# One addition per step moved from VectorE to an accumulating transfer, and the last whole-float32 products with w_out split in two

## The chip, the cores and the metric

The kernel runs on one core of a Trainium2 chip. The metric is the device time of one execution in microseconds (us); lower is better. Five engines matter here: TensorE (PE in the profile, its weight loads PEld), VectorE (DVE), ScalarE (ACT), GpSimd (POOL) and SyncE (SP). Each takes its instructions strictly in the order of the program and waits on semaphores for the others. SyncE and GpSimd here mostly issue transfers. Only GpSimd issues the transfers that add to their destination.

## The reference, cut to what matters

Attention over 8 batches and 8 heads gives `x` with 4608 rows and 512 columns. Behind it comes a feed-forward layer whose activation is a ratio of two polynomials:

```
h = x @ w_in                               # 4608x512 @ 512x2048
P = a[0] + a[1]*h + a[2]*h*h + a[3]*h*h*h  # the numerator
Q = 1 + |b[0]|*|h| + |b[1]|*h*h            # the denominator
g = P / (Q + 1e-6)
out = g @ w_out                            # 4608x2048 @ 2048x512
```

All inputs and outputs are float32.

## The kernel before, in words

The 4608 rows of `x` are cut into nine blocks of 512: eight hold the first 512 rows of a batch, the ninth the last 64 rows of all batches. A block takes 16 steps, one for each 128 columns of `h`, so there are 144 steps in all. Step n has three parts.

- H(n): TensorE makes 128 columns of `h` for the block's 512 rows, in one PSUM bank. In the first `NAT = 16` steps, which are block 0, it does so with whole float32 operands (L897): 4 instructions of the program, 8 records in the profile. From step 16 on both factors are split into a high and a low part, and three of the four products of the parts are summed (L909): 12 instructions.
- middle(n): four passes of ScalarE over the bank give `tb` = |b0 h|, `tq` = h², `ta` = a3 h + a2 and `u` = a1 h + a0. VectorE makes `tb` = b1 h² + |b0 h| (L937), `ta` = `ta` times `tq` (L942) and `ta` = `ta` + `u` (L943), which is P. ScalarE takes a logarithm and an exponential, `tq` = 1/Q. Then VectorE makes `gh` = `ta` times `tq` in the rounded format that TensorE takes at its faster rate (L949) and, in three more instructions (L952, L957, L958), the correction `gl`.
- O(n): TensorE multiplies `gh` and `gl` with the two parts of the matching 128 rows of w_out, 12 instructions (L989), and adds them to four PSUM banks that hold the block's output. In the first `WO = 4` steps it multiplies the whole float32 quotient with whole w_out instead: one VectorE instruction (L947) writes the quotient over `u`, and O(n) is 4 instructions (L970), 8 records.

The tiles are few and shared. Step n uses the set of its parity: `m0`, `m2`, `m4` are `ta`, `tb`, `tq` of even steps, `m1`, `m3`, `m5` of odd ones. `gb0` and `gb1` are `u`, and they are the same memory as `g0` and `g1`, which are `gh`; likewise `gb2`, `gb3` (the logarithm) and `g2`, `g3` (`gl`). So ScalarE can write `u` of step n only after O(n-2) has read `gh` of step n-2, and `ta` only after L957 of step n-2. H(n) alternates between two banks from step 2 on and needs its bank read out by all four passes of step n-2.

Around the steps runs the rest: attention for the coming block (its scores are L692, the pooled ones L467), the weights, which come as eight megabyte-sized loads for each of w_in and w_out (SP L344), each unpacked by one ScalarE and two VectorE instructions (L351, L354, L357) and split by one of each (L371, L374), and the pooled inputs of attention, which GpSimd sums by accumulating transfers (L419).

Every piece of work is entered in a list with its engine, an assumed duration, what it reads and writes, a due time and a lag until its readers can go on. A planner (`Plan.run`) plays this list through and takes the open task with the earliest latest start on each engine; its order is the order of the program. `H_FIRST` is the spacing of due times for the steps of block 0, `H_STEP` that of the others. In the lists below a name such as `g0_122` is tile `g0` with a number of the allocator; `wh1`, `wl1` and `wb1` are the high part, the low part and the whole of w_out, `wb0` the whole of w_in, `xf0_1` is `x` of block 0, `sx` and `sl` are places where loads land.

Of the kernel before, what the change touches and what calls it, by code (L numbers as in the profile page):

```python
# [14 lines left out]
ALU = mybir.AluOpType  # L15
# [9 lines left out]
POOL = 4  # L25
# [48 lines left out]
class Plan:  # L74
# [11 lines left out]
    def add(self, engine, dur, fn, reads=(), writes=(), due=None, lag=None):  # L86
        t = Task()
        t.engine, t.dur, t.fn, t.due, t.n = engine, dur, fn, due, len(self.tasks)
        t.lag, t.preds, t.succs, t.late, t.start = lag, {}, [], 1e9, None
        rk = set().union(*(r.keys for r in reads)) if reads else set()  # L90
        wk = set().union(*(w.keys for w in writes)) if writes else set()
        for k in rk | wk:
            w = self.writer.get(k)
            if w is not None:
                t.preds[w] = True
        for k in wk:
            for r in self.readers.get(k, ()):
                t.preds.setdefault(r, False)
            self.writer[k] = t
            self.readers[k] = []  # L100
        for k in rk - wk:
            self.readers[k].append(t) if k in self.readers else self.readers.__setitem__(k, [t])
        t.preds.pop(t, None)
        for p in t.preds:
            p.succs.append(t)
        self.tasks.append(t)
        return t
# [75 lines left out]
def attention_moe(  # L183
# [13 lines left out]
    nc = tc.nc  # L197
# [3 lines left out]
    add = plan.add  # L201
# [136 lines left out]
    def weights(w, f, spot, due=None):  # L338
# [26 lines left out]
        add("DVE", 1.13, lower, (spot, lo), (lo,))  # L365
        if f >= (WO if w else NAT):
            parts(w, f)

    def parts(w, f, due=None):
        hi, lo, word = high2[w][f // 2], low2[w][f // 2], bits2[w][f // 2]  # L370
        add("ACT", 0.88, lambda: nc.scalar.copy(out=hi.ap, in_=word.ap.bitcast(F32)), (lo,), (hi,), due=due)  # L371
        add(
            "DVE", 1.13,
            lambda: nc.vector.tensor_tensor(  # L374
                out=lo.ap, in0=word.ap.bitcast(F32), in1=hi.ap.bitcast(F32), op=ALU.subtract
            ),
            (lo, hi), (lo,), due=due,
        )
# [152 lines left out]
    def normalize(c):  # L531
# [22 lines left out]
        else:  # L554
            add("ACT", 0.92, pooled, (*c.eproom, s.sm), c.eproom, lag=LATE)
        add(
# [3 lines left out]
            ),  # L560
            (s.el, s.sm), (s.el,), lag=None if c.b == 0 else LATE,
        )
# [289 lines left out]
    def due_h(n):  # L852
        m = blocks[0].nstep
        return H0 + H_FIRST * min(n, m) + H_STEP * max(0, n - m)

# [26 lines left out]
    def bank_h(n):  # L882
        return banks[HFIRST[n]] if n < len(HFIRST) else hb[n % 2]
# [37 lines left out]
    def act(cost, out_, room_in, in_, func, *more, **kw):  # L921
        add("ACT", cost, lambda: nc.scalar.activation(out=out_.ap, in_=in_, func=func, **kw), (room_in, cf, *more), (out_,))  # L922

    def middle(n):

        ta, tb, tq = (mt[2 * i + n % 2] for i in range(3))
        gh, gl = gt[n % 2], gt[2 + n % 2]
        u, log = gb[n % 2], gb[2 + n % 2]
        h = bank_h(n)
        act(0.58, tb, h, h.ap, AF.Abs, scale=b0)  # L930
        act(0.48, tq, h, h.ap, AF.Square)
        act(0.66, ta, h, h.ap, AF.Identity, scale=a3, bias=a2)
        act(0.66, u, h, h.ap, AF.Identity, scale=a1, bias=a0)
        v = nc.vector
        add(
            "DVE", 0.66,
            lambda: v.scalar_tensor_tensor(  # L937
                out=tb.ap, in0=tq.ap, scalar=b1, in1=tb.ap, op0=ALU.mult, op1=ALU.add
            ),
            (tq, tb, cf), (tb,),  # L940
        )
        add("DVE", 0.61, lambda: v.tensor_tensor(out=ta.ap, in0=ta.ap, in1=tq.ap, op=ALU.mult), (ta, tq), (ta,))  # L942
        add("DVE", 0.61, lambda: v.tensor_tensor(out=ta.ap, in0=ta.ap, in1=u.ap, op=ALU.add), (ta, u), (ta,))  # L943
        act(0.63, log, tb, tb.ap, AF.Ln, bias=cone)
        act(0.54, tq, log, log.ap, AF.Exp, scale=-1.0)
        if n < WO:
            add("DVE", 0.61, lambda: v.tensor_tensor(out=u.ap, in0=ta.ap, in1=tq.ap, op=ALU.mult), (ta, tq), (u,))  # L947
            return
        add("DVE", 0.61, lambda: v.tensor_tensor(out=gh.ap, in0=ta.ap, in1=tq.ap, op=ALU.mult), (ta, tq), (gh,))  # L949
        add(  # L950
            "DVE", 0.61,
            lambda: v.scalar_tensor_tensor(  # L952
                out=tb.ap, in0=tb.ap, scalar=CONE, in1=gh.ap.bitcast(F32), op0=ALU.add, op1=ALU.mult
            ),
            (tb, gh), (tb,),
        )
        add("DVE", 0.61, lambda: v.tensor_tensor(out=tb.ap, in0=ta.ap, in1=tb.ap, op=ALU.subtract), (ta, tb), (tb,))  # L957
        add("DVE", 0.61, lambda: v.tensor_tensor(out=gl.ap, in0=tb.ap, in1=tq.ap, op=ALU.mult), (tb, tq), (gl,))  # L958

    def o_part(n, f):  # L960
# [4 lines left out]
        due = due_h(n) + O_LAG * H_STEP + 0.25 * f  # L965
        if n < WO:
            for sub in range(blk.nsub):
# [120 lines left out]
    for n in range(NS + LAG):  # L1088
        if n < NS:
            k, s = steps[n]  # L1090
            for f in range(blocks[k].fg):
                h_part(n, f)
                if n < NAT:
                    if n % 2:
                        parts(0, n - 1, due_h(n - 1 + blocks[0].nstep) - 2.0)
                    if n == NAT - 1 and NAT < blocks[0].nstep:
                        split_x(0, due_h(NAT) - 3.0)
            if s == blocks[k].nstep - 1:

                if k + 1 < len(blocks):  # L1100
                    split_x(k + 1)
        o = n - LAG
        if o >= 0:
            k, s = steps[o]
            for f in range(blocks[k].fg):
                o_part(o, f)
            if s == blocks[k].nstep - 1:
                store(k)
                if blocks[k].b is not None and blocks[k].b + 2 < B:
                    attend(blocks[k].b + 2)  # L1110

        if n < NS:
            middle(n)
# [10 lines left out]
    for t in pe:  # L1124
        n = int(WARM * (t.start - end) / 0.107)
# [18 lines left out]
LAG = 2  # L1144
O_LAG = 2.11
H0 = 7.65
H_FIRST = 7.02
H_STEP = 6.3
SPLIT_EARLY = 9.51
QUAD_GAP = 37.85  # L1150
WARM = 0.6
EP_DVE = (0,)
WO = 4
SPOTS = (0, 1, 2, 3, 4, 5)
LATE = 1.2


_OUTS = [((NT, DM), "float32")]
# [65 lines left out]
```

## Time and profile before

| what | us |
|---|---|
| median of 3 runs | 971.54 (971.37 to 972.34) |
| time of the profiled execution | 972.59 |
| its span, first to last instruction | 970.70 |
| PE busy | 945.7 (97%) |
| DVE busy | 847.4 (87%) |
| ACT busy | 817.8 (84%) |
| POOL busy | 112.2 (12%) |

The span is the time that the profile covers; 1.89 us of the profiled execution lie around it. A timeline row gives start, busy time, engine, source line, operation, tiles and shape, and how many instructions were merged; a bracket tells how long the engine was idle before it and what ended that. Successive records of one engine overlap in these rows, so the price of an instruction is the distance between starts, not the busy time.

### The profile page before, as it was taken

The numbers are of one execution on the slowest core, as the hardware profiler recorded it, in microseconds if no ns is written. First come the engines' busy times: TensorE is split into PE (matmuls) and PEld (weight loads), VectorE is DVE, ScalarE is ACT, GpSimd is POOL, SyncE is SP. The second block draws the span as 40 slices with busy tenths as digits, with TensorE's granted clock in tenths as the row PEclk, the third lists the DMA queues.
The fourth block names the chain that finished last, engine by engine and source line by source line (L and its number), as shares of the span: only waits on it lengthen the run. The fifth ranks groups of instructions, "written<-read, shape, count | busy, mean of one in ns | idle before, by whom it ended". The sixth has DMA issues, their size and how long they took to land.

```text
span 970.7 us, 19136 instructions
## 1 busy us (share of the span) xinstructions
PE 945.7 (97%) x7077; PEld 738.4 (76%) x7077; DVE 847.4 (87%) x1438; ACT 817.8 (84%) x2054; POOL 112.2 (12%) x135
## 2 busy tenths in 40 slices
PE   4999999999999999999999999999999999999996
PEld 3745656887887788778877888778877888888885
DVE  5789999999897989898988889798989899988885
ACT  5799998998879897889788988988798977778774
POOL 1210121021202120112102210212021000000000
PEclk7799999999999999999999999999999999999998
DMA  9994463235424433344223532344242010001001
GB/s 311 273 330 136 110 152 62 94 57 120 78 77 75 107 57 93 81 98 78 68 96 55 122 72 83 60 119 66 71 94 63 1 44 1 1 1 44 1 1 44
DMA packets 43013, 84.85 MB, mean 87 GB/s; under 512 B 4872, under 2 KB 25736, under 8 KB 42920
## 3 DMA queue, kind: packets, MB, share of 16 engines
q1 hardware_dynamic: 25256, 63.42, 19.7%
q0 software_dynamic: 17664, 20.21, 15.2%
q8 instruction: 56, 0.92, 0.4%
q14 instruction: 37, 0.30, 0.1%
HBM read 74.17 MB, written 9.44 MB: 86 GB/s over the span
## 4 chain that ended last, share of the span: by engine, by line
PE 53%; DVE 22%; ACT 17%; issue 5%; DMA 2%; DVEq 0%; ACTq 0%
PE psum L989 23%; PE psum L909 21%; ACT el L727 5%; ACT m L922 5%; DVE g L949 3%; DVE m L952 3%; DVE m L957 3%; PE psum L605 2%; ACT gb L922 2%; DVE g L958 2%; DVE m L942 2%; DMA qk<-in_qk_dram 2%; DVE m L937 2%; DVE m L943 2%; ACT epc L523 2%
## 5 line engine op out<-in xcount | busy, mean ns | idle before, releaser
L989 PE MATMUL psum<-wh,g 128*128 128x512 f32 x1120 | 379.4, 401 | 1.8 <-DVE g L958 1.7
L909 PE MATMUL psum<-xs,wh 128*128 128x512 f32 x1024 | 261.6, 395 | 0.1
L922 ACT ACTIVATE m<-psum,cf 128x512 f32<-128x512 f32 x288 | 211.9, 741 | 58.5 <-PE psum L909 54.9
L989 PEld LDWEIGHTS psum<-wh,g 128*128 128x128 f32 x1120 | 208.0, 188 | 53.8 <-DVE g L958 4.7
L909 PEld LDWEIGHTS psum<-xs,wh 128*128 128x128 f32 x1024 | 189.3, 188 | 43.6 <-issue 2.9
L989 PE MATMUL psum<-wl,g 128*128 128x512 f32 x560 | 218.0, 390 | 0.0
L949 DVE TENSOR_TENSOR g<-m,m 128x512 fp32r<-128x512 f32 x140 | 96.6, 690 | 72.5 <-ACT m L922 66.7
L909 PE MATMUL psum<-xs,wl 128*128 128x512 f32 x512 | 137.0, 389 | 0.0
L922 ACT ACTIVATE gb<-psum,cf 128x512 f32<-128x512 f32 x144 | 114.9, 798 | 15.4 <-PE psum L989 15.4
L922 ACT ACTIVATE gb<-m,cf 128x512 f32<-128x512 f32 x144 | 106.4, 739 | 22.0 <-DVE m L937 19.7
L989 PEld LDWEIGHTS psum<-wl,g 128*128 128x128 f32 x560 | 105.2, 188 | 21.8 <-issue 1.4
L419 POOL DMA_DIRECT2D pq<-in_qkp_dram x84 | 73.7, 922 | 398.7 <-DMA pq<-in_qkp_dram 385.5
L922 ACT ACTIVATE m<-gb 128x512 f32<-128x512 f32 x144 | 92.6, 643 | 24.7 <-DVE m L942 22.5
L909 PEld LDWEIGHTS psum<-xs,wl 128*128 128x128 f32 x512 | 96.1, 188 | 20.3
L937 DVE SCALAR_TENSOR_TENSOR m<-m,cf,m 128x512 f32<-128x512 f32 x144 | 107.3, 745 | 1.6 <-ACT m L922 1.6
L943 DVE TENSOR_TENSOR m<-m,gb 128x512 f32<-128x512 f32 x144 | 98.9, 687 | 7.0 <-DVE m L942 0.5
L952 DVE SCALAR_TENSOR_TENSOR m<-m,g 128x512 f32<-128x512 f32 x140 | 96.5, 690 | 3.7
L942 DVE TENSOR_TENSOR m<-m,m 128x512 f32<-128x512 f32 x144 | 98.4, 683 | 0.0
L958 DVE TENSOR_TENSOR g<-m,m 128x512 fp32r<-128x512 f32 x140 | 95.8, 685 | 2.8
L957 DVE TENSOR_TENSOR m<-m,m 128x512 f32<-128x512 f32 x140 | 96.2, 687 | 2.1
L727 ACT ACTIVATE el<-el,nm 128x64 f32<-128x64 f32 x280 | 93.4, 340 | 2.8 <-DVE nm L721 2.8
L922 ACT ACTIVATE m<-psum 128x512 f32<-128x512 f32 x144 | 87.0, 604 | 0.0
(84 smaller groups left out, 924.9 us busy)
## 6 DMA issues: line engine op xcount, KB each, us to landing
qk<-in_qk_dram SPq DMA_DIRECT2D x32, 590.0 KB, 3.9
pq<-in_qkp_dram POOLq DMA_DIRECT2D x84, 144.0 KB, 3.3
vw<-in_vw_dram SPq DMA_DIRECT2D x32, 320.0 KB, 3.8
out_dram<-xf SPq DMA_DIRECT2D x32, 256.0 KB, 2.6
vpc<-in_vp_dram POOLq DMA_DIRECT2D x42, 168.0 KB, 3.8
sx<-in_w_in_dram SPq DMA_DIRECT2D x5, 1024.0 KB, 13.4
sl<-in_w_out_dram SPq DMA_DIRECT2D x4, 1024.0 KB, 7.0
sx<-in_w_out_dram SPq DMA_DIRECT2D x4, 1024.0 KB, 4.9
```

The lines of the kernel that those rows point to most:

```text
L419: lambda d=dst, x=x: nc.gpsimd.dma_start(out=d.ap, in_=x, accum_op=ALU.add),
L727: nc.scalar.activation(out=e[:, n], in_=e[:, n], func=AF.Exp, bias=nm[:, n : n + 1], scale=scale, accum_out=sm[:, n : n + 1],)
L909: nc.tensor.matmul(ph.ap[:, f * t : (f + 1) * t], lhsT=(high, low)[j][0][fc].ap[:, c, :], rhs=blk.x[i].ap[:, c, :] if blk.b is not None el ...
L922: add("ACT", cost, lambda: nc.scalar.activation(out=out_.ap, in_=in_, func=func, **kw), (room_in, cf, *more), (out_,))
L937: lambda: v.scalar_tensor_tensor(out=tb.ap, in0=tq.ap, scalar=b1, in1=tb.ap, op0=ALU.mult, op1=ALU.add),
L942: add("DVE", 0.61, lambda: v.tensor_tensor(out=ta.ap, in0=ta.ap, in1=tq.ap, op=ALU.mult), (ta, tq), (ta,))
L943: add("DVE", 0.61, lambda: v.tensor_tensor(out=ta.ap, in0=ta.ap, in1=u.ap, op=ALU.add), (ta, u), (ta,))
L949: add("DVE", 0.61, lambda: v.tensor_tensor(out=gh.ap, in0=ta.ap, in1=tq.ap, op=ALU.mult), (ta, tq), (gh,))
L952: lambda: v.scalar_tensor_tensor(out=tb.ap, in0=tb.ap, scalar=CONE, in1=gh.ap.bitcast(F32), op0=ALU.add, op1=ALU.mult),
L957: add("DVE", 0.61, lambda: v.tensor_tensor(out=tb.ap, in0=ta.ap, in1=tb.ap, op=ALU.subtract), (ta, tb), (tb,))
L958: add("DVE", 0.61, lambda: v.tensor_tensor(out=gl.ap, in0=tb.ap, in1=tq.ap, op=ALU.mult), (tb, tq), (gl,))
L989: nc.tensor.matmul(ob[sub].ap, lhsT=g[i].ap[:, f0 : f0 + P], rhs=flat((high, low)[j][1][fc].ap), start=(fc == 0 and m == 0), stop=(fc == N ...
```

## The change

In steps 0 to 15 the VectorE addition `ta` + `u` becomes a transfer, issued by GpSimd, that adds `u` to `ta`; the planner is told 0.95 us on GpSimd and a lag of 4.0 us. `WO = 0` makes O(0) to O(3) split products, with the four VectorE instructions for `gh` and `gl`, and has the parts of their w_out rows made when the weights are unpacked. `H_FIRST` becomes 6.39. The source lines behind the change move by 3.

```
-        add("DVE", 0.61, lambda: v.tensor_tensor(out=ta.ap, in0=ta.ap, in1=u.ap, op=ALU.add), (ta, u), (ta,))
+        if n < UN:
+            add("POOL", 0.95, lambda: nc.gpsimd.dma_start(out=ta.ap, in_=u.ap, accum_op=ALU.add), (ta, u), (ta,), lag=ULAG)
+        else:
+            add("DVE", 0.61, lambda: v.tensor_tensor(out=ta.ap, in0=ta.ap, in1=u.ap, op=ALU.add), (ta, u), (ta,))
...
-H_FIRST = 7.02
+H_FIRST = 6.39
...
-WO = 4
+WO = 0
...
+ULAG = 4.0
+UN = 16
```

On TensorE, before, the end of H(0) to H(3) is followed by O(0) and O(1) in whole float32, with the scores of attention between them, and then by the first half of H(4):

```order
L897 MATMUL psum<-xf0_1_107,wb0_2_75 128x512 x6
L970 MATMUL psum<-wb1_0_89,gb0_126 128x512 x4
L692 MATMUL psum<-qk0_148 64x64 x20
L970 MATMUL psum<-wb1_0_89,gb1_127 128x512 x4
L897 MATMUL psum<-xf0_1_107,wb0_4_77 128x512 x2
```

The same place on TensorE now (three equal pairs on `g0_122` and three on `g1_123` follow those shown, and are left out):

```order
L897 MATMUL psum<-xf0_1_107,wb0_2_75 128x512 x6
L692 MATMUL psum<-qk0_148 64x64 x20
L992 MATMUL psum<-wh1_0_64,g0_122 128x512
L992 MATMUL psum<-wl1_0_88,g0_122 128x512
L992 MATMUL psum<-wh1_0_64,g2_124 128x512 x4
L992 MATMUL psum<-wh1_0_64,g1_123 128x512
L992 MATMUL psum<-wl1_0_88,g1_123 128x512
L897 MATMUL psum<-xf0_1_107,wb0_4_77 128x512 x2
L992 MATMUL psum<-wh1_0_64,g3_125 128x512 x4
```

The scores moved ahead of O(0), and O(0) now needs `gh` first and `gl` (`g2_124`) before O(1) and H(4) can come.

On VectorE, before, the middle of steps 0 and 1, from the first addition to the second quotient:

```order
L943 TENSOR_TENSOR m0_116<-m0_116,gb0_126 128x512
L374 TENSOR_TENSOR wl0_0_72<-wb0_0_73,wh0_0_56 128x1024
L947 TENSOR_TENSOR gb0_126<-m0_116,m4_120 128x512
L937 SCALAR_TENSOR_TENSOR m3_119<-m5_121,cf_134,m3_119 128x512
L942 TENSOR_TENSOR m1_117<-m1_117,m5_121 128x512
L937 SCALAR_TENSOR_TENSOR m2_118<-m4_120,cf_134,m2_118 128x512
L943 TENSOR_TENSOR m1_117<-m1_117,gb1_127 128x512
L354 TENSOR_SCALAR wb1_2_91<-sl2_183 128x1024
L947 TENSOR_TENSOR gb1_127<-m1_117,m5_121 128x512
```

The same stretch on VectorE now, from the two products to `gl` of step 0:

```order
L942 TENSOR_TENSOR m0_116<-m0_116,m4_120 128x512
L937 SCALAR_TENSOR_TENSOR m2_118<-m4_120,cf_134,m2_118 128x512
L942 TENSOR_TENSOR m1_117<-m1_117,m5_121 128x512
L374 TENSOR_TENSOR wl0_0_72<-wb0_0_73,wh0_0_56 128x1024
L937 SCALAR_TENSOR_TENSOR m3_119<-m5_121,cf_134,m3_119 128x512
L952 TENSOR_TENSOR g0_122<-m0_116,m4_120 128x512
L354 TENSOR_SCALAR wb1_2_91<-sl2_183 128x1024
L955 SCALAR_TENSOR_TENSOR m2_118<-m2_118,g0_122 128x512
L357 SCALAR_TENSOR_TENSOR wb1_2_91<-sl2_183,wb1_2_91 128x1024
L960 TENSOR_TENSOR m2_118<-m0_116,m2_118 128x512
L952 TENSOR_TENSOR g1_123<-m1_117,m5_121 128x512
L961 TENSOR_TENSOR g2_124<-m2_118,m4_120 128x512
```

Both L943 are gone, four instructions for `gh` and `gl` stand in place of one L947, and two instructions of the weights as well as `gh` of step 1 stand between `gh` and `gl` of step 0.

On GpSimd the transfers of steps 0 to 5 now stand among those of attention:

```order
L419 DMA vpc_162<-in_vp_dram 112x384
L944 DMA m0_116<-gb0_126 128x512
L944 DMA m1_117<-gb1_127 128x512
L419 DMA vpc_162<-in_vp_dram 112x384
L944 DMA m0_116<-gb0_126 128x512
L944 DMA m1_117<-gb1_127 128x512
L944 DMA m0_116<-gb0_126 128x512
L419 DMA pq0_149<-in_qkp_dram 128x288
L419 DMA pq1_156<-in_qkp_dram 128x288
L944 DMA m1_117<-gb1_127 128x512
```

The row ahead of the first L944 is the second accumulation of `vpc`; that of step 5 stands behind the first ones of `pq0` and `pq1`, the second half of attention.

## The prediction, made before the changed kernel ran

> **What bounds the kernel now.** I read the page first, then the table by stage, then TensorE's timeline through block 0, then the engines that feed it.
>
> ```profile
> PE 945.7 (97%) x7077; PEld 738.4 (76%) x7077; DVE 847.4 (87%) x1438; ACT 817.8 (84%) x2054; POOL 112.2 (12%) x135
> 41.00:65.00 24.00, 23.98 (x222) 13.18 (x217) 17.63 (x29) 19.46 (x32) 5.16 (x6) 1.00 1.02 328
> 65.00:83.00 18.00, 18.00 (x81) 8.17 (x80) 17.47 (x25) 17.73 (x42) 0.00 (x0) 1.00 0.47 160
> 83.00:159.00 76.00, 74.89 (x573) 47.10 (x573) 73.13 (x127) 72.44 (x192) 14.70 (x17) 1.00 0.53 125
> 136.34 2.84 PE L897 MATMUL psum<-xf,wb 128*128 128x512 f32 x6 [1.11 <-ACT gb L922]
> ```
>
> The rows of stages give start and end, length, then busy time of PE, PEld, DVE, ACT and POOL with counts, the granted clock, the share of time in which the transfer engines were busy, and GB/s. TensorE has no idle time from 41 to 83 us, and from 83 to 159 us, where block 0 ends, 1.11 us, the single wait in the last row. VectorE and ScalarE are almost as full from 65 us on, but TensorE does not wait for them: it is the bound, and an instruction less on VectorE buys nothing by itself. Only TensorE work that goes, or a TensorE wait that comes or goes, moves the end. The program's order on TensorE is the same in both kernels from early in block 1 to the end, so a shift gained or lost in block 0 is carried to the end unchanged.
>
> This is TensorE where block 0 starts, the place that the change alters most:
>
> ```profile
> 51.58 8.85 PE L897 MATMUL psum<-xf,wb 128*128 128x512 f32 x20
> 60.27 3.60 PE L970 MATMUL psum<-wb,gb 128*128 128x512 f32 x8
> 63.79 0.81 PE L692 MATMUL psum<-qk 64*64 64x64 f32 x40
> 64.62 3.70 PE L970 MATMUL psum<-wb,gb 128*128 128x512 f32 x8
> 68.16 1.88 PE L897 MATMUL psum<-xf,wb 128*128 128x512 f32 x4
> 69.88 1.88 PE L970 MATMUL psum<-wb,gb 128*128 128x512 f32 x4
> 71.59 1.02 PE L897 MATMUL psum<-xf,wb 128*128 128x512 f32 x2
> 812.98 2.72 PE psum L989 x12
> ```
>
> H(0) to H(3) end at 60.27, O(0) follows at once, then the scores of attention (0.83 us from start to start), O(1), and H(4) at 68.16.
>
> **The change part by part.** *TensorE's work.* From 68.16 to 69.88 to 71.59, four whole-float32 records take 1.715 us, so an O(n) of 8 records takes 3.43. The last row is from the chain that ended last: a split O(n), 12 records, takes 2.72. Four steps save 4 x (3.43 - 2.72) = **2.84 us**. That is all TensorE saves.
>
> *VectorE's work.*
>
> ```profile
> 51.54 0.89 DVE L646 TENSOR_TENSOR xf<-psum,up 128x464 f32<-128x464 f32 x3 [3.17 <-PE psum L605]
> 65.07 1.23 DVE L357 SCALAR_TENSOR_TENSOR wb<-sl,wb 128x1024 int32<-128x1024 int32 x1
> 66.21 0.70 DVE L943 TENSOR_TENSOR m<-m,gb 128x512 f32<-128x512 f32 x1
> 66.81 0.83 DVE L705 TENSOR_TENSOR el<-psum,maskd 128x640 f32<-128x640 f32 x1
> 69.41 0.70 DVE L354 TENSOR_SCALAR wb<-sl 128x1024 int32<-128x1024 int32 x1
> 70.01 0.70 DVE L943 TENSOR_TENSOR m<-m,gb 128x512 f32<-128x512 f32 x1
> ```
>
> From start to start, L943 costs 0.60 us, L354 0.60 and L357 1.14; I price the other 512-wide operations at 0.60 too. Sixteen additions go (-9.6 us), three instructions come in each of steps 0 to 3 (+7.2): 2.4 us less, on an engine that TensorE was not waiting for. I cost this at nothing. The parts of the first w_out rows (two L371, two L374) are made earlier; the first L374 falls into an idle 3.17 us of VectorE just ahead of 51.54, the second is one of the instructions between steps 2 and 3 below.
>
> *The chain of step 0.* O(0) now waits for `gh`, and that for the transfer.
>
> ```profile
> 54.46 0.69 ACT L922 ACTIVATE m<-psum,cf 128x512 f32<-128x512 f32 x1 [2.11 <-PE psum L897]
> 55.05 0.59 ACT L922 ACTIVATE m<-psum 128x512 f32<-128x512 f32 x1
> 55.52 0.78 ACT L922 ACTIVATE m<-psum,cf 128x512 f32<-128x512 f32 x1
> 56.19 0.79 ACT L922 ACTIVATE gb<-psum,cf 128x512 f32<-128x512 f32 x1
> 56.85 0.73 ACT L922 ACTIVATE gb<-m,cf 128x512 f32<-128x512 f32 x1
> 57.46 0.79 ACT L922 ACTIVATE m<-psum,cf 128x512 f32<-128x512 f32 x1
> 58.13 0.64 ACT L922 ACTIVATE m<-gb 128x512 f32<-128x512 f32 x1
> 58.65 0.79 ACT L922 ACTIVATE gb<-psum,cf 128x512 f32<-128x512 f32 x1
> ```
>
> ScalarE starts on the bank at 54.46, when H(0) is done; nothing in the change moves that. By these starts a pass costs 0.59 (`tb`), 0.47 (`tq`), 0.67 (`ta`), 0.66 (`u`), 0.61 (logarithm), 0.52 (exponential). In the new order `ta`, `tq`, `u` come first, so `u` is written at 54.46 + 0.67 + 0.47 + 0.66 = 56.26 and VectorE's product at about 56.3: GpSimd can issue at **56.5**. Before `gh` of step 0, VectorE also has L937 of step 1, which needs the tenth pass, `tb` of step 1: the sum of ten such passes, 5.9 us, ends at 60.4, and with 0.1 for a semaphore and 0.60 for L937 `gh` can start at **61.1** at the earliest, however fast the transfer is.
>
> How long the transfer takes is the unknown.
>
> ```profile
> 49.49 0.86 POOL L419 DMA_DIRECT2D vpc<-in_vp_dram  x1 [0.16 <-issue]
> 57.83 0.82 POOL L419 DMA_DIRECT2D vpc<-in_vp_dram  x1 [7.48 <-DMA vpc<-in_vp_dram]
> DMA to landing us min/median/max: 3.3/7.1/8.2
> 56.00:60.00 4.00, 4.00 (x11) 1.85 (x10) 3.46 (x5) 4.00 (x8) 0.82 (x1) 1.00 1.03 398
> 60.00:64.00 4.00, 4.00 (x22) 1.57 (x24) 3.36 (x6) 4.00 (x8) 0.00 (x0) 1.00 1.05 359
> DMA to landing us min/median/max: 3.2/3.5/8.2
> vpc<-in_vp_dram POOLq DMA_DIRECT2D x42, 168.0 KB, 3.8
> 53.71 0.41 SPq L344 DMA_DIRECT2D sx<-in_w_in_dram  x1
> ```
>
> The first landing row is of the accumulating transfers issued from 30 to 60 us, the second of those in the whole run. While the weights load, they need 7.1 us (median) instead of 3.5. The second accumulation of `vpc`, issued at 49.49, held GpSimd until 57.83, 8.3 us, and the transfer engines stay full to 64 us. The new transfer is issued just into this, and is larger: 256 KB against 168. The change moves one megabyte (the load at 53.71) behind two other loads, but it stood last in its queue, so what is ahead of the transfer is the same. Ends: 3.3 us from an empty queue, 9 us with the larger size; nearest is the 8.3 us row, and I take **8.0**. `gh` of step 0 then starts at T = 56.5 + 8.0 = 64.5.
>
> *TensorE's waits.* With the scores ahead of O(0), TensorE is through at 60.27 + 0.83 = 61.1. O(0) can start at T + 0.7 (`gh`, 0.60, and a semaphore): a wait of T - 60.4. Its first eight records last 1.81 us, to T + 2.5. Then it needs `gl`, and VectorE does L354, L955, L357, L960, `gh` of step 1 and L961 first: 0.60 x 6 + 1.14 after `gh` started plus 0.06, T + 4.8. A second wait of 2.3. O(1) cannot run ahead of it and H(4) needs its bank read by ScalarE, whose `tb` of step 2 needs the old `tb` free after L961, at about T + 6.3; TensorE, with O(0) and O(1) before it, comes there at T + 7.6. So I see no third wait. Sum of the waits: **T - 58.1**, 6.4 us at T = 64.5. The transfer of step 1 is issued 2.9 us later (its `u` is ready at 59.3) and its `gh` is due at T + 3.6, so the same landing time is enough there.
>
> *Steps 2 and 3, and 4 to 15.* `u` of step 2 follows O(0)'s `gh` records, `gh` of step 2 stands behind 11 instructions of VectorE, some 7.4 us by the prices above, and comes at about T + 12.2, and TensorE, with H(4), the rest of O(1), scores and a quarter of H(5) to do, reaches O(2) at T + 13.6: hidden, by 1.4 us, with the weights' L374 (1.14, as L357) included. From step 4 on, the rest of O(n-2), two H and one O, 0.91 + 2 x 3.43 + 2.72 = 10.5 us without attention, lie on TensorE between the moment when `u` may be written and O(n), against 0.66 for `u`, 0.86 for the issue, 3.5 for the landing and 0.60 for `gh`, 5.6: hidden, with 4.9 us for what each queue has ahead. GpSimd does its queue in order; the transfer of step 5 waits for the plain `pq` load behind the pooled scores, which ends about when `u` of step 5 is written: nothing added. The 1.11 us at 136.34 is ScalarE's, crowded by attention's exponentials in both orders; I leave it, with 1.1 us either way for such waits.
>
> *Sum.* -2.84 + 6.4 = **+3.6 us**. On the profiled execution, 972.59 with a span of 970.70, that is 976.2 and 974.3; it lies 1.05 above the median of the runs, so for the median I say 971.54 + 3.6 = **975.1 us**.
>
> The Trainium skill, "DMA: Bandwidth & Descriptors", section "Anatomy of one DMA — SWDGE (gpsimd) path", gives about 2.0 us plus bytes over 436 GB/s, an estimate of 2.6 us for 256 KB. By that rule the first rival below holds; the trace does not agree, its fastest such transfer takes 3.2 us for 144 KB, and 7 to 8 beside the weights.
>
> **The rivals.** *A: the transfer lands early.* If it needs under 4.6 us, T is at its floor of 61.1, the waits are 3.0 and the sum +0.16; with the wait of 1.11 gone, -0.95. That is 970.6 to 971.7, no change. For it: 3.3 us is seen as soon as the queue is empty. Against it: the queue is full to 64 us. It decides between slower and not at T = 62.8, a landing in 6.3 us.
>
> *B: the clock drops in the wait.*
>
> ```profile
> 8.00:10.00 2.00, 1.71 (x88) 1.53 (x79) 1.60 (x3) 0.51 (x4) 0.85 (x1) 1.00 1.02 254
> 10.00:12.00 2.00, 0.29 (x1) 0.10 (x1) 0.69 (x3) 2.00 (x15) 0.99 (x2) 1.00 1.01 409
> 12.00:14.00 2.00, 0.00 (x0) 0.00 (x0) 1.64 (x3) 2.00 (x15) 0.00 (x0) 0.55 1.07 365
> 32.00:36.00 4.00, 4.00 (x47) 3.86 (x44) 2.77 (x9) 2.13 (x7) 1.80 (x2) 0.50 1.02 400
> 36.00:38.00 2.00, 2.00 (x13) 1.24 (x13) 1.09 (x2) 1.88 (x6) 0.00 (x0) 0.97 1.06 298
> ```
>
> With 0.29 us of work in four, TensorE's clock went to half after 12 us and stayed there to 36. The new wait, 4.1 us with nothing in it, is of that length. O(0)'s first records at half speed still end before `gl` comes; if the clock then stays low for 4 us of steady work, as from 32 to 36 us, half of that time is lost: +2.0, **977.1**. Against it: nothing shows how much idle time it takes with large matmuls before it. The Trainium skill, "TensorE: Matmul & The Clock Gate", Part 1, says that an idle window of about 3.4 us halves the clock; the rows agree that a gap of this size can, and by that rule B would need the window to fall wholly into the wait.
>
> *C: the VectorE time counts.* If VectorE, 73.13 of 76 us busy, does set the pace through waits that the rows hide in TensorE's pipelining, its 2.4 us come on top of the 2.84 and the 1.11: with T at 62 the sum is -2.84 + 3.9 - 3.5 = -2.4, 969.1. Against it stands that TensorE's records follow each other at their own price.
>
> **How the numbers follow.** The forecast 0.41, B 0.25, A 0.22, C 0.12. About 0.2% (1.9 us) is what a measurement of this kernel can tell from none. Forecast and B are slower, save landings below 6.3 us, which are A; so slower 0.65, within 0.2% 0.23, faster 0.12. The range goes from A's lower end with a little of C, 970.0, to B with a landing in 9 us, 978.5. The likeliest case alone, 6.4 to 9 us with 1.1 either way: 973 to 977.
>
> **What would show it.** Right: TensorE idle for 3 to 5 us before the first O(0) record, released by `gh` (L952), and about 2 us between O(0)'s eighth and ninth record; VectorE idle before L952 of step 0, released by the transfer; that transfer landing in 7 us or more; no new wait above 1 us after 85 us; every block from the second on as long as before. Wrong: a landing under 6 us at 56 to 65 us; the wait before O(0) under 2 us; steps 4 to 15 waiting for their transfers, which would make it slower than said; or a granted clock under 1.00 between 60 and 75 us, which is B.

## The result, and the profile after

The changed kernel takes 983.57 us (median; 981.98 to 984.32) against 971.69 us for the kernel before on the same chip: ratio 1.012 (95% interval 1.0107 to 1.0133), 11.9 us slower. The direction was forecast, the size was not: 3.6 us were said, and the range ended at 978.5. The profiled execution took 983.32 us with a span of 981.5, so 10.7 us more than the profiled one before. "Faster" and "slower" below are against the kernel before in the same comparison.

The table by stage, with the columns of the prediction and one more stretch:

```profile
41.00:65.00 24.00, 20.48 (x218) 11.67 (x217) 14.80 (x24) 19.47 (x30) 6.59 (x8) 0.98 1.05 315
65.00:83.00 18.00, 15.96 (x83) 10.09 (x84) 15.16 (x24) 12.12 (x26) 1.81 (x2) 0.83 0.86 271
83.00:159.00 76.00, 71.98 (x464) 44.52 (x466) 70.56 (x116) 72.31 (x197) 21.84 (x25) 0.98 0.63 137
139.00:147.00 8.00, 4.63 (x11) 3.14 (x11) 6.18 (x13) 8.00 (x26) 2.66 (x4) 0.79 0.29 62
```

TensorE, full before, now lacks 3.5 us in the first stage, 2.0 in the second and 4.0 in the third, most of it at 139 to 147 us, and its clock falls to 0.83 and 0.79. ScalarE, 17.73 of 18 us busy before at 65 to 83 us, has 12.12.

TensorE's waits, with the rows around them (the bracket is the wait and what ended it):

```profile
65.58 0.77 PE L992 MATMUL psum<-wh,g 128*128 128x512 f32 x1 [4.10 <-DVE g L952]
69.63 2.03 PE L992 MATMUL psum<-wh,g 128*128 128x512 f32 x5 [0.30 <-DVE g L961]
73.11 1.88 PE L897 MATMUL psum<-xf,wb 128*128 128x512 f32 x4
80.78 0.50 PE L992 MATMUL psum<-wh,g 128*128 128x512 f32 x1 [1.16 <-DVE g L952]
96.23 1.98 PE L897 MATMUL psum<-xf,wb 128*128 128x512 f32 x4 [0.65 <-ACT m L922]
142.72 0.79 PE L992 MATMUL psum<-wh,g 128*128 128x512 f32 x1 [3.37 <-DVE g L952]
146.19 1.88 PE L897 MATMUL psum<-xf,wb 128*128 128x512 f32 x4
```

The waits are O(0) for `gh`, the same for `gl`, O(2), an H, and O(10); the rows at 73.11 and 146.19 are the H that follow, and mark where slow records end. The chain of step 0 on GpSimd and VectorE, and the same of step 2:

```profile
57.34 0.90 POOL L944 DMA_DIRECT2D m<-gb  x1 [7.45 <-ACT m L922]
64.74 0.69 DVE L952 TENSOR_TENSOR g<-m,m 128x512 fp32r<-128x512 f32 x1 [3.14 <-DMA m<-gb]
73.27 0.89 POOL L944 DMA_DIRECT2D m<-gb  x1 [11.52 <-DVE m L942]
80.03 0.69 DVE L952 TENSOR_TENSOR g<-m,m 128x512 fp32r<-128x512 f32 x1 [1.47 <-DMA m<-gb]
```

The account in us: the wait of 4.10; from 65.58 to 73.11 lie 20 records that take 0.227 each at full clock, 4.54, so 2.99 more (0.30 of it the second wait, the rest half clock); 1.16; 0.65; 3.37; eight records from 142.72 to 146.19, 3.47 instead of 1.82, so 1.65. That is 13.92. Off go 2.84 saved and the old wait of 1.11, which is gone: **9.97** of the 10.7. (H(0) to H(3) also end about 0.3 us later in this execution than in that of before; the rest is not assigned.) The start of block 0 costs 7.1 where 6.4 was forecast. The wait of step 2 and the one at O(10) with its slow records, 6.2 together, were not forecast at all.

### The profile page after: what moved, and what is told of

Read it like the earlier page. It is cut to its first block, busy times and chain, and to the rows that moved or that the text cites. A ratio compares the mean times of both kernels' runs of the same rounds, so it can differ in the third digit from the quotient of the medians.

```text
span 981.5 us, 19191 instructions
## 1 busy us (share of the span) xinstructions
PE 948.0 (97%) x7093; PEld 744.6 (76%) x7093; DVE 845.9 (86%) x1434; ACT 817.3 (83%) x2054; POOL 126.5 (13%) x151
## 4 chain that ended last, share of the span: by engine, by line
PE 61%; ACT 15%; DVE 15%; DMA 5%; issue 3%; DVEq 0%; POOL 0%; ACTq 0%; POOLq 0%; SPq 0%
PE psum L992 27%; PE psum L909 24%; ACT el L727 4%; ACT m L922 4%; DMA m<-gb 3%; DVE g L952 2%; PE psum L605 2%; DVE m L955 2%; DMA qk<-in_qk_dram 2%; ACT gb L922 2%; DVE m L960 2%; DVE m L942 2%; DVE g L961 2%; PE psum L897 2%; ACT epc L523 2%
## 5 line engine op out<-in xcount | busy, mean ns | idle before, releaser
L992 PE MATMUL psum<-wh,g 128*128 128x512 f32 x1152 | 392.8, 404 | 11.3 <-DVE g L952 9.3
L992 PEld LDWEIGHTS psum<-wh,g 128*128 128x128 f32 x1152 | 215.5, 189 | 67.1 <-DVE g L952 9.9
L992 PE MATMUL psum<-wl,g 128*128 128x512 f32 x576 | 226.0, 393 | 0.0
L952 DVE TENSOR_TENSOR g<-m,m 128x512 fp32r<-128x512 f32 x144 | 99.5, 691 | 81.4 <-ACT m L922 68.8
L992 PEld LDWEIGHTS psum<-wl,g 128*128 128x128 f32 x576 | 109.4, 190 | 23.7 <-issue 2.2
L955 DVE SCALAR_TENSOR_TENSOR m<-m,g 128x512 f32<-128x512 f32 x144 | 99.3, 690 | 3.5
L961 DVE TENSOR_TENSOR g<-m,m 128x512 fp32r<-128x512 f32 x144 | 98.8, 686 | 3.4 <-DVE m L960 0.5
L960 DVE TENSOR_TENSOR m<-m,m 128x512 f32<-128x512 f32 x144 | 99.0, 688 | 2.0
L942 DVE TENSOR_TENSOR m<-m,m 128x512 f32<-128x512 f32 x144 | 98.6, 685 | 2.4 <-ACT m L922 2.4
L946 DVE TENSOR_TENSOR m<-m,gb 128x512 f32<-128x512 f32 x128 | 88.1, 688 | 6.2
```

The source lines that it names most:

```text
L955: lambda: v.scalar_tensor_tensor(out=tb.ap, in0=tb.ap, scalar=CONE, in1=gh.ap.bitcast(F32), op0=ALU.add, op1=ALU.mult),
L992: nc.tensor.matmul(ob[sub].ap, lhsT=g[i].ap[:, f0 : f0 + P], rhs=flat((high, low)[j][1][fc].ap), start=(fc == 0 and m == 0), stop=(fc == N ...
```

## The experiments

The numbers of all runs, each against the kernel before on the same chip:

| run | us | ratio, 95% interval |
|---|---|---|
| e1_same_order_vector | 978.98 | 1.0073 (1.0056 to 1.0090) |
| e2_first_two_vector | 979.88 | 1.0087 (1.0070 to 1.0105) |
| e3_split_alone | 978.57 | 1.0070 (1.0055 to 1.0085) |
| e4_transfer_alone | 991.37 | 1.0192 (1.0168 to 1.0217) |
| e5_step10_moved | 983.02 | 1.0117 (1.0103 to 1.0131) |
| e6_clock_kept | 983.28 | 1.0120 (1.0105 to 1.0136) |
| e7_old_spacing | 984.76 | 1.0135 (1.0121 to 1.0148) |
| e8_vector_moved | 980.14 | 1.0083 (1.0070 to 1.0096) |
| e9_fewer_exps | 980.59 | 1.0093 (1.0080 to 1.0107) |
| e10_before_fewer_exps | 972.63 | 1.0003 (0.9994 to 1.0012) |
| e11_split_less_vector | 978.76 | 1.0071 (1.0057 to 1.0085) |
| e12_transfers_4_to_9 | 971.25 | 0.9995 (0.9987 to 1.0004) |
| e13_chunks_due | 979.31 | 1.0076 (1.0064 to 1.0089) |
| e14_start_and_chunks | 977.03 | 1.0054 (1.0041 to 1.0068) |
| e15_late_chunks | 974.45 | 1.0027 (1.0018 to 1.0037) |
| e16_relief_only | 969.05 | 0.9968 (0.9956 to 0.9980) |
| e17_relief_same_order | 971.55 | 0.9994 (0.9985 to 1.0003) |
| e18_due_without_transfers | 969.19 | 0.9973 (0.9963 to 0.9983) |

### The order without the transfers: e1 and e2

The planner plans with transfers; what is emitted at their places is VectorE's addition (e1: in all sixteen steps; e2: `ONV = (0, 1)`).

```
+            move = lambda: nc.gpsimd.dma_start(out=ta.ap, in_=u.ap, accum_op=ALU.add)
+            if n in ONV:
+                move = lambda: v.tensor_tensor(out=ta.ap, in0=ta.ap, in1=u.ap, op=ALU.add)
+            add("POOL", 0.95, move, (ta, u), (ta,), lag=ULAG)
```

> The changed kernel's order of instructions word for word, but all sixteen additions are done by VectorE, each at the place that the planner gave its transfer; no transfer of 256 KB is left. If the waits of the changed kernel are the transfers' own (landing late, or queued behind others on GpSimd), then gh of step 0 starts at its floor of about 61.1 us, TensorE waits 0.7 + 2.3 us there, the other new waits vanish, and with 2.84 us saved the time is about 971.7 us. If the new order is at fault (twenty exponentials of attention stand ahead of the logarithm of step 10 on ScalarE), the wait of 3.4 us at O(10) and its 1.65 us at half clock stay: about 976.7 us. If ScalarE's idle time at 65 to 83 us is a debt paid at step 10, the time is as in the first case, 971 to 973 us.

> The changed kernel's order, with the additions of steps 0 and 1 alone on VectorE and the other fourteen as transfers. The waits around O(0), 7.1 us in the changed kernel, should shrink to about 3.0 us: -4.1 us, about 979.5 us, if the later waits (step 2, step 10) stand by themselves, through the transfers or through the order. If the later waits only pay for the idle time that the first wait gave ScalarE, the wait at O(10) goes too: about 974.5 us.

Without one transfer the order still costs 0.73%, 7.1 us; the transfers add the other half point, and e2 shows that most of that, 3.2 us by the ratios, belongs to steps 0 and 1 (the rest, between e1 and e2, is within the intervals). e2 came out as its first expectation: the waits of step 2 (1.10) and O(10) (4.38) stay. TensorE in e1:

```profile
61.75 0.47 PE L995 MATMUL psum<-wh,g 128*128 128x512 f32 x1 [0.87 <-DVE g L955]
65.80 1.67 PE L995 MATMUL psum<-wh,g 128*128 128x512 f32 x5 [1.97 <-DVE g L964]
138.49 0.79 PE L995 MATMUL psum<-wh,g 128*128 128x512 f32 x1 [2.71 <-DVE g L955]
```

The floor of the prediction (`gh` at 61.1, waits of 0.7 and 2.3) is confirmed by 0.87 and 1.97, with `gh` at 60.92; half clock behind the second wait, which the floor did not have, costs some 1.7 us more. The wait at O(10) stays, without any transfer.

One reserve: in e1 VectorE does sixteen additions for which this order was not planned, so the 7.1 us are the order and these additions together. At O(10) the additions are not what is waited for, since VectorE itself is idle for 1.28 us, until ScalarE is done, shortly before that `gh`. What stands ahead of this `gh` shows on ScalarE of the changed kernel:

```profile
131.23 1.17 ACT L351 ACTIVATE sx<-sx 128x1024 f32<-128x1024 f32 x1 [1.28 <-DMA sx<-in_w_out_dram]
132.29 0.34 ACT L727 ACTIVATE el<-el,nm 128x64 f32<-128x64 f32 x1
138.60 0.34 ACT L727 ACTIVATE el<-el,nm 128x64 f32<-128x64 f32 x1
138.93 0.71 ACT L922 ACTIVATE gb<-m,cf 128x512 f32<-128x512 f32 x1
```

ScalarE sits idle for 1.28 us until a weight load has landed and unpacks it; then come twenty exponentials of attention (the first and the last are shown), and only then the logarithm of step 10. In the kernel before, the exponential of the pending step stood ahead of them.

### Each part alone: e3, e4 and e7

e3 is the kernel before with `WO = 0`; e4 with the sixteen transfers; e7 the changed kernel with `H_FIRST = 7.02`. The planner orders anew each time.

> The kernel before with the split products of O(0) to O(3) alone; additions on VectorE, spacing of due times 7.02 as before; the planner orders anew. TensorE saves 2.84 us and gh of step 0 is due at about 58.8 us, ahead of TensorE's 60.3, so no wait: 968.7 us if VectorE's time costs nothing. If VectorE sets the pace too, its twelve added instructions (7.2 us, against 3.4 us of idle time that it has between 65 and 159 us) show: 971.5 to 975.3 us, slower than before.

> The kernel before with the sixteen transfers alone; O(0) to O(3) whole, spacing 7.02; the planner orders anew. Nothing is saved on TensorE. The wait ahead of O(0) is about 4.1 us, no gl is needed there: 975.6 us if the rest hides; 980 us or more if the transfers of later steps are waited for as in the changed kernel; under 971 us only if VectorE's 9.6 us fewer count.

> The changed kernel with the spacing of due times put back to 7.02 (the planner orders anew; transfers and split products stay). If the spacing of 6.39 wrote the bad order, the 7.4 us that the order costs with all additions on VectorE go for the most part: about 976.5 us. If the split products and transfers make it, whatever the spacing, 983 us or more.

Each part alone is slower, and the spacing is not the culprit. e3 came out above both of its expectations. In it, nothing waits for `gh` of step 0, as expected, but the same picture as above stands at another place: exponentials from 85.69 to 92.35 ahead of a logarithm, and then TensorE.

```profile
92.35 0.71 ACT L922 ACTIVATE gb<-m,cf 128x512 f32<-128x512 f32 x1
```

```profile
96.13 0.50 PE L992 MATMUL psum<-wh,g 128*128 128x512 f32 x1 [4.03 <-DVE g L952]
142.04 2.84 PE L897 MATMUL psum<-xf,wb 128*128 128x512 f32 x6 [2.68 <-ACT gb L922]
```

In e4 TensorE waits 4.09 us before O(0) as expected, but also 3.40 before another whole O, 1.38 and 2.92, with slow records behind three of them.

### The three instructions of step 10: e5 and e8

In the changed kernel's order (e5), and in e1's (e8), three entries of step 10 (`EARLY = (10,)`) are moved: logarithm and exponential ahead of the exponentials of attention, as far as what they read allows, which is behind the first five, and `gh` ahead of the normalisation.

```
+    for n in EARLY:
+        log, ex, gh = TAG[n]
...
+        put_at(log, first)
+        put_at(ex, todo.index(log) + 1)
...
+        put_at(gh, first)
```

> The changed kernel with three instructions moved: ScalarE's logarithm and exponential of step 10 stand ahead of the twenty exponentials of attention (6.6 us) instead of behind them, and gh of step 10 ahead of the normalisation that waits for ScalarE. gh(10) can then start at about 137.3 us instead of 141.98, before TensorE comes to O(10) at 139.5, so the wait of 3.4 us there goes. If the place of these three is the whole cause, nothing waits instead: -3.4 and -1.65 of half clock, about 978.5 us. If ScalarE has simply fallen behind and its place in the order only shows it, its four passes of step 11 still come at 142.2 to 144.7 us, H(13) waits for them in place of O(10), and the gain is about 1.5 us: 982 us.

> The changed kernel's order with all sixteen additions on VectorE (979.0 us) and the same three instructions of step 10 moved. By the place alone: the wait of 2.9 us at O(10) and its 1.7 us at half clock go, about 974.5 us. By a ScalarE that is behind: H(13) waits instead, gain about 1.5 us, 977.5 us.

No gain: 983.02, close to the second expectation of e5, and 980.14, above both of e8. The wait at O(10) is gone and stands at H(13), which needs ScalarE's passes of step 11. This is TensorE, then ScalarE, of e5:

```profile
144.47 3.49 PE L899 MATMUL psum<-xf,wb 128*128 128x512 f32 x4 [5.02 <-ACT m L924]
```

```profile
130.80 1.16 ACT L353 ACTIVATE sx<-sx 128x1024 f32<-128x1024 f32 x1 [2.59 <-DMA sx<-in_w_out_dram]
143.72 0.70 ACT L924 ACTIVATE m<-psum,cf 128x512 f32<-128x512 f32 x1
```

So the place of the three is not the cause: ScalarE comes late to all that stands there. It sat idle for 2.59 us until a late load had landed (first row), and from then on it went without a pause through the unpacking, the exponentials and the passes, to the last pass of step 11 (second row).

### The clock: e6

36 small matmuls fill the wait ahead of O(0).

```
+            if t is first_o:
+                warm(36)
```

> The changed kernel with 36 small matmuls (128x256, results overwritten) on TensorE ahead of O(0), so that TensorE is busy in its wait of 4.1 us and its clock should stay at 1.00. If the clock matters there (rival B of the prediction), about 2 us are gained: 981.6 us. If O(0) at half clock is covered by the wait for gl, which comes at 69.6 us in any case, only the five slow records behind gl are gained: 0.6 to 1.0 us, 982.8 us.

```profile
41.00:65.00 24.00, 24.00 (x226) 14.64 (x223) 15.76 (x25) 18.63 (x27) 5.64 (x7) 1.00 1.07 327
68.47 1.57 PE L992 MATMUL psum<-wh,g 128*128 128x512 f32 x5 [2.03 <-DVE g L961]
71.00:72.00 1.00, 1.00 (x4) 0.71 (x4) 1.00 (x2) 1.00 (x3) 0.54 (x1) 0.50 1.00 410
```

O(0) ran at full clock, but `gl` came no earlier: TensorE waited 2.03 us for it, and behind that wait the clock halved all the same, until 73 us. So e6 moves the half clock instead of avoiding it, and does not price rival B. TensorE reached O(10) no sooner (102.2 us after it began H(0), in both executions) and waited 4.61 us there instead of 3.37; the time did not change (983.28).

### ScalarE's load: e9 and e10

The twenty exponentials become four, in the changed kernel and in the one before; the row sums are left out there, and five rows share one maximum.

```
+            def one(lo):
+                nc.scalar.activation(
+                    out=e[:, lo : lo + NW // 2], in_=e[:, lo : lo + NW // 2], func=AF.Exp,
+                    bias=nm[:, lo : lo + 1], scale=scale,
+                )
...
+                do = one if c.b == 1 and c.i // 2 == 1 else exps
```

> The changed kernel in its own order, with the twenty exponentials of attention ahead of the logarithm of step 10 (6.6 us of ScalarE) replaced by four over five groups each, without their sums; that part of the softmax is not computed. It takes some 4.9 us from ScalarE at the one place. If ScalarE's load there makes the wait at O(10), O(10) and H(13) both come without a wait: -3.4 -1.65, about 978.5 us. If something else comes as late (the transfers of steps 10 and 11, VectorE), the time stays above 981 us.

> Control for the run above: the kernel before with the same twenty exponentials replaced by four. There TensorE waits 1.1 us for ScalarE at that place (136.34 us), so at most 1.3 us can be gained: 970.4 us. If ScalarE's total work set the pace of the kernel before, 4.9 us would be gained: 966.7 us.

Before, nothing is gained (1.0003): ScalarE's total work does not set the pace. TensorE's old wait stays too, at 1.13 us, and ScalarE then waits 2.70 us for VectorE shortly ahead of it. In the changed kernel 3.0 us come back (983.57 to 980.59; 2.6 by the ratios), not 5.0, and a wait of 2.33 us is left at O(10). VectorE of e9, and a row of its ScalarE, show what stands next in the way:

```profile
132.69 1.29 DVE L354 TENSOR_SCALAR wb<-sx 128x1024 int32<-128x1024 int32 x2
133.90 2.36 DVE L357 SCALAR_TENSOR_TENSOR wb<-sx,wb 128x1024 int32<-128x1024 int32 x2
137.07 0.38 ACT L523 ACTIVATE epc<-psum,nm 128x144 f32<-128x144 f32 x1 [2.67 <-DVE nm L517]
139.52 0.69 DVE L959 TENSOR_TENSOR g<-m,m 128x512 fp32r<-128x512 f32 x1
```

Two pairs of L354 and L357, the unpacking of two weight chunks, take 3.5 us of VectorE; its L517 comes behind them, ScalarE waits 2.67 us for that, and the exponential of step 10 stands behind this wait. They lie there because of what happened to the loads. SP and ScalarE in the kernel before, then in the changed one:

```profile
75.09 0.37 SPq L344 DMA_DIRECT2D sx<-in_w_out_dram  x1
82.27 0.37 SPq L344 DMA_DIRECT2D sx<-in_w_in_dram  x1
110.83 0.38 SPq L344 DMA_DIRECT2D sx<-in_w_out_dram  x1
73.86 1.19 ACT L351 ACTIVATE sx<-sx 128x1024 f32<-128x1024 f32 x1
85.52 1.14 ACT L351 ACTIVATE sx<-sx 128x1024 f32<-128x1024 f32 x1
```

```profile
68.27 0.46 SPq L344 DMA_DIRECT2D sx<-in_w_in_dram  x1
68.78 0.47 SPq L344 DMA_DIRECT2D sx<-in_w_out_dram  x1
119.33 0.38 SPq L344 DMA_DIRECT2D sx<-in_w_in_dram  x1
123.79 0.38 SPq L344 DMA_DIRECT2D sx<-in_w_out_dram  x1
113.71 2.20 ACT L351 ACTIVATE sx<-sx 128x1024 f32<-128x1024 f32 x2
```

These are the twelfth and the thirteenth chunk. Before, they are loaded at 53.71 (a row of the prediction) and 75.09, and ScalarE unpacks them at 73.86 and 85.52. Now both are loaded at 68 us and unpacked only at 113.71. The next two chunks go to the same two places, which come free late: their loads leave at 119.33 and 123.79 (before, 82.27 and 110.83), and their unpacking falls among the exponentials and the middles of steps 9 to 11.

### VectorE's added work: e11

e3 without eight of its twelve added VectorE instructions, which leaves the correction `gl` of steps 0 to 3 uncomputed.

```
+        few = n < 4
...
+            lambda: None if few else v.scalar_tensor_tensor(
```

> The kernel with the split products alone (978.6 us) in its own order, with eight of its twelve added VectorE instructions left out (L955 and L960 of steps 0 to 3; the correction gl is then not computed rightly). That is 4.8 us less for VectorE at 59 to 75 us, where it has no idle time. If VectorE's added work made the split products slower, most of it comes back: about 974 us. If the place of ScalarE's exponentials made it (a wait of 4.2 us at 96 us and one of 2.8 us at 142 us), under 1.5 us comes back: 977.5 us.

978.76 against 978.57: nothing comes back, and TensorE waits 3.27 and 3.41 us at the two places of e3. In that order VectorE's work is not what TensorE waits for.

### The chunks: e13, e14 and e15

e13 is the changed kernel with a due time for two chunks, e14 keeps steps 0 and 1 on VectorE besides, e15 has transfers in steps 2 to 11, `WO = 2`, `H_FIRST = 6.3` and no due time.

```
+        soon = 55 if order.index((w, f)) in (11, 12) else None
-        add("ACT", 0.94, scaled, (spot,), (spot,))
...
+        add("ACT", 0.94, scaled, (spot,), (spot,), due=soon)
...
```

The two VectorE instructions get the same due time.

> The changed kernel, with a due time for the unpacking of two weight chunks (the twelfth and thirteenth), which the planner otherwise leaves until 113 us; the planner orders anew, transfers and split products stay. If their late unpacking makes the wait at O(10), that wait (3.4 us and 1.65 us at half clock) goes: about 978.5 us. If the engines' idle time in the first wait is a debt that has to be paid somewhere, another wait takes its place: 982 us or more.

> As the run with the due time, and the additions of steps 0 and 1 stay on VectorE (transfers in steps 2 to 15; the planner knows it). By the two causes together, 5.0 us for the late chunks and 3.7 us for the first wait: about 975 us. If the split products' twelve added VectorE instructions cost by themselves, 978 us or more.

> Transfers in steps 2 to 11, O(2) and O(3) split, O(0) and O(1) whole, spacing 6.3; the planner unpacks the fourteenth and fifteenth chunk late, as in the changed kernel. If late chunks cost whatever stands around them, 974 us or more. If only their meeting with the exponentials ahead of a logarithm costs, 970 us, since 1.4 us of TensorE are saved.

e13 gives back 4.3 us, close to its first expectation. The next two loads left at 97.61 and 99.91; at 139 to 147 us no wait above 0.3 us is left, and none at step 2. These are its waits above half a microsecond between O(0) and 175 us:

```profile
93.77 1.98 PE L898 MATMUL psum<-xf,wb 128*128 128x512 f32 x4 [0.56 <-ACT m L923]
109.37 0.50 PE L993 MATMUL psum<-wh,g 128*128 128x512 f32 x1 [1.65 <-DVE g L953]
113.04 0.73 PE L993 MATMUL psum<-wh,g 128*128 128x512 f32 x2 [0.71 <-DVE g L962]
```

That supports the late chunks as the cause; the planner moved other work too, so the due time is not isolated. e14 came to 977.03, not 975: its first wait is gone, but TensorE waits five times for 1.0 to 1.6 us between 64 and 105 us, for `gh`, for `gl`, for a pass of ScalarE and for an unpacking. e15's time is near the first expectation, but its trace refutes it: its only wait above 0.3 us before 165 us is 2.59 us for `gl` at 83.67; the late chunks (loads at 128.44 and 129.64), which meet no pending logarithm, cost nothing that can be seen.

### Away from the start: e12, e16, e17 and e18

e12 and e16 have transfers in steps 4 to 9 alone (`UN = 10`), with `WO = 4` and `H_FIRST = 6.3`; e16 adds the due time and plans a lag of 6.0. e17 is e16's order with its additions on VectorE; e18 has the due time and the spacing, and is planned without transfers.

```
-        if n < UN:
+        if 4 <= n < UN:
```

> The kernel before with transfers in steps 4 to 9 alone (O(0) to O(3) whole, spacing of due times 6.3; the planner orders anew). Nothing waits for a transfer at the start of block 0, and VectorE has 3.6 us less. If the cost of the change lies in the start and in VectorE's added work, this is no slower than before, 968 to 972 us. If a new order and transfers beside the loads of the weights cost by themselves, 975 us or more.

> The kernel before with transfers in steps 4 to 9 alone (a lag of 6 us for the planner), the due time for the two chunks, and spacing 6.3. VectorE has 3.6 us less and TensorE as much as before, so only the wait of 1.1 to 1.3 us at step 12 of the kernel before can be gained, as in the run without the due time: 970.5 us; under 969 us if VectorE's relief counts beyond that.

> The order of the fastest version so far (transfers in steps 4 to 9, the two chunks due early; 0.9968 of the kernel before) with its six additions done by VectorE at the places of the transfers. If VectorE's relief carries the gain, up to 3.6 us come back: 971 to 972.5 us. If the order alone carries it, the time stays at 969 us.

> The kernel before with the due time for the two chunks and the spacing of 6.3, no transfer at all; the planner orders anew. If the due time and the spacing carry the gain of the fastest version, 969 us; if the transfers do, 971 us or more.

e12 is no slower than the kernel before (0.9995), with no TensorE wait in block 0, although the same two loads leave late in it too, at 112.61 and 116.81. So neither transfers away from the start nor late chunks cost by themselves, which e15 says of the chunks too; what they meet must matter, and no run isolates that. e16 is the fastest kernel of this study, 0.32% under the kernel before, also with no TensorE wait in block 0; e18 has the same without a transfer, and the two lie within each other's intervals. This is the stretch from 83 to 159 us in e16, e17 and e18, in this order:

```profile
83.00:159.00 76.00, 76.00 (x572) 48.22 (x565) 73.39 (x125) 75.21 (x183) 19.74 (x22) 1.00 0.63 139
```

```profile
83.00:159.00 76.00, 75.10 (x570) 46.23 (x563) 74.77 (x129) 73.75 (x181) 14.66 (x17) 1.00 0.50 116
```

```profile
83.00:159.00 76.00, 76.00 (x562) 49.01 (x561) 75.15 (x131) 73.85 (x180) 15.41 (x18) 1.00 0.50 117
```

In one and the same order (e16, e17) six additions on VectorE cost 2.5 us; 0.9 of it is two waits of TensorE (75.10 of 76.00 us busy), the rest is not assigned. An order made for VectorE needs no transfer.

## Why the prediction was right in direction and wrong in size

- **TensorE's saving, 2.84 us**: the trace has the split O(n) at 0.227 us a record. But e3, which has this saving and none of the transfers, is 0.70% slower, 6.8 us: what comes with the saving costs more than three times as much.
- **The chain of step 0**: right in mechanism, and the close agreement is in part luck. The transfer was issued at 57.34 (said: 56.5) and `gh` started at 64.74 (said: 64.5), 7.4 us later where 8.0 was said: two misses that nearly cancel. The wait before O(0) was 4.10 (said: 4.1). Rival A needed a landing under 6.3 us and falls.
- **The second wait, 2.3 us**: 2.99, since half clock filled it and went on behind it. That is rival B in part, at 0.7 us instead of 2.0 at this place, since most of the half clock fell into the second wait; e6 could not test it further.
- **Steps 2 and 3, "hidden, by 1.4 us"**: wrong. `gh` of step 2 came at 80.03, 15.3 us after T where 12.2 was said, and O(2) waited 1.16 us. The 12.2 counted VectorE's instructions; what came last was the landing of the transfer, which left only at 73.27, behind a late L942.
- **Steps 4 to 15, "hidden, with 4.9 us"**: the step that failed. The transfers' landings were hidden; O(10) waited 3.37 us and lost 1.65 to the clock, 5.0 together, for a reason that the step didn't cost: the new order of ScalarE and VectorE. All that the prediction allowed for such waits was 1.1 us either way. e1 prices that order, with its additions on VectorE, at 7.1 us where rival A, which has the same floor, gave +0.16; the wait at O(10), which there too is for ScalarE, is 2.71 us of it, with half clock behind it.
- **"The parts of the first w_out rows are made earlier", at nothing, and "an instruction less on VectorE buys nothing"**: too simple. ScalarE and VectorE were as full as TensorE from 65 us on; that was read, and then treated as slack. When the planner lays two unpackings some 40 and 29 us later, the two behind them meet other work and TensorE waits. Rival C (VectorE's time counts) is seen between e16 and e17, not in e11.
- **"The 1.11 us at 136.34 is ScalarE's, crowded by attention's exponentials"**: not borne out. In e10 sixteen of the twenty are gone and the wait stays, at 1.13.
- **GpSimd's queue, nothing added**: no run shows a loss from it. Step 11's transfer left at 145.23, about 1 us after VectorE's product was ready, and O(11) did not wait.
- **The carry**: right; in the changed kernel less than 1 us was lost behind block 0.
- **The range's upper end**: B with a landing in 9 us adds up to 978.1 by the prediction's own terms, not 978.5.

Not settled: which single cost of the split products makes up what is left in e14 (ratio 1.0054), how much of e13's gain is the due time alone, what e16 and e18 gain over e12, none of which waits in block 0, and why the planner leaves the two chunks so late.

## What to carry to other kernels

Where three engines are over 95% busy and a planner orders them, a change of a few instructions is first of all a new order: price it by running the new order with the old operations, before pricing the operation. A wait that moves to the next consumer when its instructions are moved ahead points to an engine that comes late to the whole stretch rather than to a misplaced instruction; look for what was put off into it. And a transfer in place of an addition costs its landing wherever nothing else is left to do, as at the start of a block.

## What the runs showed of the hardware

- **A wait of 2 us can be enough to halve TensorE's clock, and the loss can come when the wait is over.** These are stretches of e1 (wait from 63.83 to 65.80) and of the changed kernel (wait from 139.35 to 142.72):

```profile
64.00:66.00 2.00, 0.20 (x1) 0.20 (x2) 2.00 (x4) 2.00 (x4) 0.00 (x0) 1.00 0.41 78
66.00:67.00 1.00, 1.00 (x5) 0.81 (x5) 1.00 (x2) 1.00 (x2) 0.00 (x0) 0.92 0.95 389
67.00:70.00 3.00, 3.00 (x9) 2.33 (x8) 2.67 (x6) 2.67 (x4) 0.00 (x0) 0.50 1.02 419
70.00:72.00 2.00, 2.00 (x7) 0.95 (x6) 2.00 (x3) 1.93 (x4) 0.00 (x0) 0.94 1.03 422
```

```profile
139.00:142.00 3.00, 0.35 (x1) 0.00 (x0) 1.18 (x4) 3.00 (x14) 0.89 (x1) 1.00 0.27 92
142.00:143.00 1.00, 0.28 (x1) 0.28 (x2) 1.00 (x4) 1.00 (x4) 0.00 (x0) 0.82 0.56 65
143.00:146.00 3.00, 3.00 (x8) 2.32 (x9) 3.00 (x6) 3.00 (x8) 0.77 (x2) 0.50 0.19 30
```

  In both, the clock reads 1.00 during the wait; about 3 us after its start it halves, for some 3.4 us, and then it is full again. Neither the delay nor the length that it takes is fixed. In the wait of 4.10 us before O(0) the clock fell 2.7 us after the start, still inside the wait, and stayed low for 6.8 us; behind the wait of 4.38 us in e2 it fell only 5.3 us after the start. Waits of 1.97 (e1), 2.03 (e6) and 2.33 us (e9) were followed by half clock; waits of 2.34 (e7) and 2.68 us (e3) left it at 1.00. The Trainium skill, "TensorE: Matmul & The Clock Gate", Part 1, says that an idle window of about 3.4 us throttles, that a busy one of the same length releases, and that the windows run freely; the length of the slow stretches agrees with the second, but a wait of 1.97 us, shorter than a window, was enough here.
- **How long an accumulating transfer took to land went more with what was under way than with its size.** The new one has 256 KB:

```profile
pq<-in_qkp_dram POOLq DMA_DIRECT2D x84, 144.0 KB, 3.3
m<-gb POOLq DMA_DIRECT2D x16, 256.0 KB, 4.0
```

  The medians differ by 0.7 us, while the sixteen alone range from 3.3 to 7.3 us, and the first, beside the weights, needed the 7.3.
